# Attention with decay and a gated spatial block: weight conversion in larger blocks, later marks, two homes for operands, other sums

## Chip, cores and metric

The kernel runs on one NeuronCore of a Trainium2 chip. The metric is the device time of one execution in microseconds. Five engines work side by side, each through its own instructions in order: PE (matmul; its weight loads are listed as PEld), DVE (vector), ACT (scalar), POOL (GpSimd) and SP, which here only issues DMAs.

## The reference

Inputs are q, k, v of 8 batches x 8 heads x 576 positions x 64, a decay f, and the weights of a gated block. Cut to what is computed:

```python
scores = q @ k.T / 8 + (cum[:, None] - cum[None, :])     # cum = cumsum(log f), causal mask
attn = exp(scores - max); attn = attn / (sum(attn) + 1e-9)
x = (attn @ v), the 8 heads side by side                   # 576 x 512 per batch
h = relu(x @ w_in); u, v2 = h[:, :512], h[:, 512:]
v_n = (v2 - mean) / sqrt(var + 1e-6)
v_s = w_spatial @ v_n + b_spatial
out = (u * v_s) @ w_out                                    # 576 x 512 per batch
```

The weights `w_in` and `w_out` come as 64-bit floating point numbers.

## The kernel before

**Attention** goes by pairs of heads, 32 pairs P, four to a batch. For a pair and each of its two heads h, `scores(P, h)` multiplies four blocks of 128 queries by 128, 256, 384 and 512 keys into PSUM (tile `sc`); DVE scales, masks and takes the negated row maximum (L264, into `tt`, maximum `nm`), ACT takes the exponential with its row sum (L266, sum into `sm`), DVE adds 1e-9 to the sums and inverts them (L269, L270), and POOL multiplies `tt` by the inverse (L274). `scores_tail(P)` does the last 64 queries of both heads together in two halves of 288 keys (L285), whose maxima are joined by L289 before the exponential L290. `transposes` turns `tt` by PE (L320, tile `tp`), `evac` copies it to SBUF (L305 in float32, L309 and L310 in two parts), and `attend` multiplies by v (tile `x`) and writes the result as a high and a low part, `xh` and `xl` (L368, L369). In the program the scores of pair P+1 stand between the transposes of pair P, so the two interleave.

**Two kinds of operands.** Pairs 0 to 3 (`NQ`) use float32 score operands of 66 rows, tile `tf`: 64 rows of q and k and two decay rows from `r0`. Pairs from 4 on use two tiles `ta` and `tb` built by six DMAs per head from the parts `hi` and `lo` that `split` makes (L207, L210, L212), with decay rows from DRAM, written once by `split_rows` (L113). Pairs 0 to 4 (`NF`) have float32 attention weights `ef`, later ones `eh` and `el`.

**The gated block**, `moe(b)`, runs once per batch: five tiles through the second half of `w_in` (tiles `winh`, `winl`) with a normalisation each, then `u` through its first half, then the spatial product, then `w_out` (`woh`, `wol`). A loop hands out steps of attention and of `moe(b)` by estimated progress, with attention a quarter of a batch ahead.

**Weight conversion.** `load64` takes a block of 64-bit weights to two float32 parts: a DMA (L137), ACT for the absolute value (L141), five steps on DVE (L142, L144, L145, L147, L148), an addition on POOL (L149), ACT's copy to the high part (L150), POOL's subtraction for the low one (L151). `load_first` converts the second half of `w_in` in four blocks of 512 columns, and `w_spatial`, while pair 0 and 1 run. `load_rest` converts the first half of `w_in` in 8 blocks of 256 elements per partition before the first `moe`, and `w_out` in 8 such blocks inside `moe(0)`.

**What sets the order.** The program is written step by step, but a scheduler with its own estimates of duration places the instructions of every engine; `after(i, mark)` only keeps an instruction behind a marked earlier one. At the start PE runs 26 matmuls on a zero tile (`zm`).

Of the kernel before, what the change touches and what calls it, by code (L numbers as in the profile page):

```python
# [38 lines left out]
def attn_gmlp_kernel(ctx: ExitStack, tc: tile.TileContext, qk, v, f, w_in, w_sp, b_sp, w_out, out):  # L39
# [67 lines left out]
    def split_rows(ws, r0):  # L107
# [5 lines left out]
        SY.dma_start(out=rows_d[:], in_=f32(rt[:]))  # L113
# [21 lines left out]
    def load64(src, dh, dl, raw, w, a, mark=None):  # L135
# [5 lines left out]
        A.activation(af, hi.bitcast(F32), AF.Abs)  # L141
# [11 lines left out]
    def load_first(ws):  # L153

        for c in range(NJ):
# [25 lines left out]
    def load_rest(n, w_v, dh, dl, tag, bufs):  # L181

        raw = mo.tile([128, NJ, 64, 2], U32, name="w64", tag=("gt0", "gt1", "o")[n % 3], bufs=1)
        w = mo.tile([128, NJ, 64], U32, name="w32", tag=tag, bufs=bufs)
        t = mo.tile([128, NJ, 64], U32, name="wa", tag=tag, bufs=bufs)
        c = slice(64 * n, 64 * n + 64)
        load64(w_v[:, :, c, :], dh[:, :, c], dl[:, :, c], raw, w[:], t[:])
# [11 lines left out]

    vts, tab, parts, r0s = {}, {}, {}, []  # L200

    def split(P):
# [12 lines left out]
    def prep(P, h):  # L215

        p = slice(64 * h, 64 * h + 64)
        if P < NQ:
# [58 lines left out]
    def scores_tail(P):  # L277
        nm = wk.tile([128, 4], F32, name="nm", tag="nm", bufs=3)
        sm = wk.tile([128, 4], F32, name="sm", tag="sm", bufs=3)
        for j in range(2):  # L280
# [95 lines left out]
    def attention(b, ws=None):  # L376
        for P in range(b * PPB, (b + 1) * PPB):
            if P == 0:
# [235 lines left out]
```

## Time and profile before

| | |
|---|---|
| median of 3 runs | 815.25 us (813.65 to 815.45) |
| span of the profiled execution | 811.5 us |
| PE busy | 788.3 us (97%) |
| DVE, ACT, POOL busy | 567.1, 535.2, 478.1 us |

The profiled execution is known by its span from the first to the last instruction; the median of the timed runs lies 3.75 us above it. Busy PE time counts a matmul from its start to a modelled end, and ends overlap the next start, so a rate is read from the distance of starts.

### The profile page before, as it was taken

Reading aid. Unit: us, or ns where it says so; the run is one execution under the profiler, and the core shown is the slowest. Engines: PE = TensorE matmul, PEld = TensorE weight load, DVE = VectorE, ACT = ScalarE, POOL = GpSimd, SP = SyncE. Lnnn points to the kernel's source line nnn. Section 1 sums busy time; section 2 is a strip of 40 time slices with the busy share of each in tenths; the row PEclk is TensorE's granted clock in tenths of the full one; section 3 lists DMA queues with packets and bytes.
Section 4 is the critical chain, followed back from the end, with each engine's and each line's share of the span. In section 5 each row is a group of like instructions: output and inputs, shape, how many; then the busy total and the mean of one; then the engine's idle time right before and its main releaser. Section 6 shows DMA issues by size and latency. Waiting matters only on the chain.

```text
span 811.5 us, 15566 instructions
## 1 busy us (share of the span) xinstructions
PE 788.3 (97%) x4980; PEld 704.9 (87%) x4980; DVE 567.1 (70%) x1726; ACT 535.2 (66%) x1432; POOL 478.1 (59%) x677
## 2 busy tenths in 40 slices
PE   7999899999999999999999999999999999999997
PEld 3676678998899989998799989999899988999996
DVE  5879989676976668766776668776786658765321
ACT  5587668676776667666686667776687657764431
POOL 4767788655766647555775537566675547643151
PEclk8699999999999999999999999999999999999999
DMA  7547754456545554565554565556554664430001
GB/s 201 143 121 208 197 140 116 120 151 165 139 122 135 135 146 117 128 166 140 125 141 112 150 152 126 123 144 151 131 130 107 163 164 111 95 77 14 27 1 66
DMA packets 47476, 103.50 MB, mean 128 GB/s; under 512 B 6961, under 2 KB 15153, under 8 KB 47330
## 3 DMA queue, kind: packets, MB, share of 16 engines
q1 hardware_dynamic: 47074, 101.98, 49.8%
q8 instruction: 40, 0.66, 0.3%
q10 hardware_dynamic: 320, 0.52, 0.3%
q14 instruction: 42, 0.34, 0.1%
HBM read 39.41 MB, written 10.68 MB: 62 GB/s over the span
## 4 chain that ended last, share of the span: by engine, by line
PE 87%; DVE 5%; POOL 2%; ACT 2%; DMA 2%; issue 1%; SPq 0%; ACTq 0%; POOLq 0%; DVEq 0%
PE ps L198 47%; PE sc L198 16%; PE x L198 12%; PE tp L320 8%; PE tp L198 2%; PE tp L333 2%; DMA out_dram<-o 1%; POOL tt L274 1%; DVE w L145 1%; ACT tt L266 1%; DVE tt L264 1%; DVE eh L342 0%; DVE wa L142 0%; DVE ef L305 0%; DMA w<-in_dram 0%
## 5 line engine op out<-in xcount | busy, mean ns | idle before, releaser
L274 POOL TENSOR_SCALAR tt<-tt,sm 128x128 f32<-128x128 f32 (+3 forms) x256 | 138.3, 558 | 94.7 <-DVE sm L270 86.4
L264 DVE CUSTOM_DVE_ANT_0 tt<-sc,zm 128x128 f32<-128x128 f32 (+3 forms) x256 | 122.4, 485 | 82.4 <-PE tp L320 63.0
L309 ACT CAST eh<-tp 128x512 fp32r<-128x512 f32 (+1 forms) x270 | 111.5, 425 | 87.2 <-PE tp L320 52.5
L266 ACT ACTIVATE tt<-tt,nm 128x128 f32<-128x128 f32 (+3 forms) x256 | 144.4, 565 | 26.5 <-DVE nm L264 21.5
L310 DVE TENSOR_TENSOR el<-tp,eh 128x512 fp32r<-128x512 f32 (+1 forms) x270 | 127.9, 485 | 25.0 <-ACT eh L309 22.8
L320 PE MATMUL tp<-ident,tt 128*128 128x128 f32 x640 | 113.7, 280 | 1.3 <-DVE ef L305 0.6
L198 PE MATMUL sc<-ta 128*128 128x128 f32 (+1 forms) x336 | 107.8, 327 | 3.9 <-DVE nm L264 3.8
L198 PE MATMUL x<-eh,vt 128*128 128x320 f32 (+4 forms) x378 | 104.5, 287 | 2.7 <-POOL vt L243 1.8
L198 PE MATMUL sc<-tb 68*128 68x128 f32 (+1 forms) x336 | 104.6, 316 | 0.0
L212 POOL TENSOR_TENSOR lo<-raw,hi 128x640 fp32r<-128x640 f32 (+1 forms) x56 | 83.2, 1506 | 18.5 <-ACT hi L210 18.4
L505 POOL TENSOR_TENSOR gl<-u,gh 128x256 fp32r<-128x256 f32 x64 | 47.2, 738 | 79.3 <-ACT gh L504 76.1
L198 PE MATMUL x<-el,vt 128*128 128x256 f32 x324 | 93.4, 306 | 0.0
L320 PEld LDWEIGHTS tp<-ident,tt 128*128 128x128 f32 x640 | 76.8, 142 | 10.9 <-ACT ef L305 1.2
L198 PEld LDWEIGHTS x<-eh,vt 128*128 128x128 f32 x378 | 71.2, 189 | 5.8 <-POOL vt L243 2.7
L198 PE MATMUL ps<-sph,vnh 128*128 128x256 f32 (+1 forms) x240 | 73.3, 306 | 0.2 <-ACT o L530 0.2
L198 PE MATMUL ps<-sph,vnl 128*128 128x256 f32 (+1 forms) x240 | 71.4, 298 | 0.0
L198 PEld LDWEIGHTS sc<-ta 128*128 128x128 f32 x336 | 63.5, 189 | 9.1 <-DVE nm L264 4.9
L198 PE MATMUL ps<-spl,vnh 128*128 128x256 f32 (+1 forms) x240 | 71.2, 296 | 0.0
L198 PE MATMUL ps<-xh,winh 128*128 128x256 f32 (+1 forms) x232 | 70.1, 302 | 0.1
L198 PE MATMUL ps<-xl,winh 128*128 128x256 f32 (+1 forms) x232 | 68.9, 297 | 0.0
L368 ACT CAST xh<-x 64x256 fp32r<-64x256 f32 (+1 forms) x128 | 49.8, 392 | 28.4 <-PE x L198 26.9
L198 PE MATMUL ps<-xh,winl 128*128 128x256 f32 (+1 forms) x232 | 68.4, 295 | 0.0
(190 smaller groups left out, 2127.8 us busy)
## 6 DMA issues: line engine op xcount, KB each, us to landing
raw<-in_dram SPq DMA_DIRECT2D x28, 608.0 KB
ta<-hi SPq DMA_DIRECT2D x56, 304.0 KB
vraw<-in_dram SPq DMA_DIRECT2D x32, 320.0 KB
tb<-hi SPq DMA_DIRECT2D x56, 160.0 KB
ta<-lo SPq DMA_DIRECT2D x56, 160.0 KB
out_dram<-o SPq DMA_DIRECT2D x32, 256.0 KB
ta<-hi SPq DMA_DIRECT2D x56, 144.0 KB
tb<-lo SPq DMA_DIRECT2D x56, 144.0 KB
```

The costliest lines, as they stand in the source:

```text
L145: V.scalar_tensor_tensor(out=w, in0=hi, scalar=0xC0000000, in1=a, op0=ALU.bitwise_and, op1=ALU.bitwise_or)
L198: T.matmul(o, l, r, start=st, stop=sp)
L212: G.tensor_tensor(out=lo[:, c], in0=raw[:, c], in1=f32(hi[:, c]), op=ALU.subtract)
L264: V.tensor_tensor_reduce(out=t, in0=sc[:, 0:n], in1=zm[:, 640 - n:640], scale=-0.125, scalar=3.0e38, op0=ALU.add, op1=ALU.min, accum_out=n ...
L266: last["exp", P, h, i] = A.activation(t, t, AF.Exp, bias=nm[:, i:i + 1], scale=-1.0, accum_out=sm[:, i:i + 1])
L274: G.tensor_scalar(out=t, in0=t, scalar1=sm[:, i:i + 1], scalar2=1.0, op0=ALU.mult, op1=ALU.mult)
L309: A.copy(h_ap, ps)
L310: V.tensor_tensor(out=l_ap, in0=ps, in1=f32(h_ap), op=ALU.subtract)
L320: T.transpose(out=tp[:, (i - c) * 128:(i - c + 1) * 128], in_=tt[h][:, TOFF[i] + 128 * c:TOFF[i] + 128 * c + 128], identity=ident)
L333: T.transpose(out=tp[:, j * 128:(j + 1) * 128], in_=tl[:, c * 128:(c + 1) * 128], identity=ident)
L368: last[P, h] = A.copy(hi, ps[m0:m0 + 64, 0:n])
L505: G.tensor_tensor(out=gl[j][:, 0:256], in0=g[:, 0:256], in1=f32(gh[j][:, 0:256]), op=ALU.subtract)
```

## The change

- `load_rest` converts the first half of `w_in` in 2 blocks of 1024 elements per partition (a pool `wu` of its own, ahead of the pool `mo`), and `w_out` in 4 blocks of 512, whose raw tile shares the tile `gt` and whose work tiles share the two `vx` buffers. The two `gt` tiles become one.
- In `load_first`, ACT's first step of block 0 stands behind the last exponential of the first head (`("exp", 0, 0, 3)`), that of the other blocks behind the second exponential of the second head; the first step of this generator is held back by 0.033.
- `split_rows` stands behind the loads of pair 1, and its DMA behind `("exp", 0, 1, 0)`. The unused call `split(1)` goes. The DMA of `raw` gets the mark `("exp", P - 2, 0, 3)`, that of the decay rows of `tb` the mark `("exp", P - 1, 0, 0)`.
- The float32 operands `tf` of even pairs live in the buffers of `ta`, those of odd pairs in those of `tb`, so that pair 1 can load while pair 0 is in use.
- The row sums go to three constant tiles `se` of 4 x 2 whose second column holds 1e-9 from the start; one TENSOR_REDUCE adds the two columns in place of L269. The second half of the tail takes the first half's maximum as its starting value, and L289 goes.

The core of the diff:

```diff
-        SY.dma_start(out=rows_d[:], in_=f32(rt[:]))
+        after(SY.dma_start(out=rows_d[:], in_=f32(rt[:])), ("exp", 0, 1, 0))
...
-        A.activation(af, hi.bitcast(F32), AF.Abs)
+        after(A.activation(af, hi.bitcast(F32), AF.Abs), behind)
...
+                   ("exp", 0, 0, 3) if c == 0 else ("exp", 0, 1, 1))
...
+    sums = [cst.tile([128, NB, 2], F32, name=f"se{n}") for n in range(3)]
+    for t in sums:
+        G.memset(t, 1.0e-9)
...
-        SY.dma_start(out=raw, in_=qk[P])
+        after(SY.dma_start(out=raw, in_=qk[P]), ("exp", P - 2, 0, 3))
...
-            ta = wk.tile([66, QK], F32, name="tf", tag="ta", bufs=2)
+            ta = wk.tile([66, QK], F32, name="tf", tag="ta" if P % 2 == 0 else "tb", bufs=2)
...
-        SY.dma_start(out=f32(tb[64:68, :]), in_=rows_v[:, P, h, :])
+        after(SY.dma_start(out=f32(tb[64:68, :]), in_=rows_v[:, P, h, :]), ("exp", P - 1, 0, 0))
...
-                                                accum_out=sm[:, i:i + 1])
+                                                accum_out=se[:, i, 0:1])
...
-        V.tensor_scalar(out=sm, in0=sm, scalar1=1.0e-9, scalar2=None, op0=ALU.add)
+        V.tensor_reduce(out=sm, in_=se, op=ALU.add, axis=AX.X)
...
-                                   in1=zm[:, 0:288] if j == 0 else zm[:, 640:928], scale=-0.125, scalar=3.0e38,
+                                   in1=zm[:, 0:288] if j == 0 else zm[:, 640:928], scale=-0.125,
+                                   scalar=nm[:, 0:1] if j else 3.0e38,
...
-        V.tensor_tensor(out=nm[:, 2:3], in0=nm[:, 0:1], in1=nm[:, 1:2], op=ALU.min)
...
-                split_rows(ws, r0s[0])
-                split(1)
...
+            if P == 0:
+                split_rows(ws, r0s[0])
...
-            for n in range(8):
-                load_rest(n, wo_v, woh, wol, 'GH', 3)
+            for n in range(4):
+                raw = mo.tile([128, NJ, 128, 2], U32, name="w64", tag="gt")
+                w, a = (mo.tile([128, NJ, 128], U32, name=k, tag="vx", bufs=2) for k in ("w32", "wa"))
+                load_rest(wo_v, woh, wol, slice(128 * n, 128 * n + 128), raw, w, a)
...
-        da, dw = 0.0, 0.0
+        da, dw = 0.0, 0.033
...
+    with tc.tile_pool(name="wu", bufs=2, reuse_waits="tile") as wu:
+        for n in range(2):
+            raw = wu.tile([128, NJ, 256, 2], U32, name="w64")
+            w, a = (wu.tile([128, NJ, 256], U32, name=k) for k in ("w32", "wa"))
+            load_rest(win_v, winh, winl, slice(256 * n, 256 * n + 256), raw, w, a)
```

Since the scheduler places everything anew, the order changes in many places. Three of them:

DVE at the start, before: from the memsets of `rt` (decay rows) to the fourth score block of pair 0, head 0 (`tt_94`); `wa` and `w_...` belong to the weight conversion.

```order
L85 MEMSET rt 32x4x64 x2
L142 TENSOR_SCALAR wa<-wa 128x512
L144 TENSOR_SCALAR wa<-wa 128x512
L264 ISA tt_94,nm<-sc,zm 128x128
L264 ISA nm 128x1
L145 SCALAR_TENSOR_TENSOR w_177<-w_176,wa 128x512
L142 TENSOR_SCALAR wa<-wa 128x512
L264 ISA tt_94,nm<-sc,zm 128x256
L264 ISA nm 128x1
L147 TENSOR_SCALAR wa<-w_177 128x512
L264 ISA tt_94,nm<-sc,zm 128x384
```

The same place after (L268 is the old L264, L289 the old L285, L273 the new sum):

```order
L85 MEMSET rt 32x4x64 x2
L268 ISA tt_94,nm<-sc,zm 128x128
L268 ISA nm 128x1
L268 ISA tt_94,nm<-sc,zm 128x256
L268 ISA nm 128x1
L268 ISA tt_94,nm<-sc,zm 128x384
L268 ISA nm 128x1
L268 ISA tt_94,nm<-sc,zm 128x512
L268 ISA nm 128x1
L289 ISA tl,nm<-sc,zm 128x288
L289 ISA nm 128x1
L273 TENSOR_REDUCE sm<-se_101 128x4
```

The conversion steps that stood ahead of the first score block, and between the blocks, now stand behind all four and the first half of the tail.

PE before, from the last score block of pair 0 to the first product with v (`x_335`); the blocks 128 and 256 behind the 512 belong to pair 1:

```order
L198 MATMUL sc<-tf 128x512
L198 MATMUL sc<-tf 128x128
L198 MATMUL sc<-tf 128x256
L320 MATMUL tp<-ident,tt_94 128x128 x3
L198 MATMUL sc<-tf 128x384
L320 MATMUL tp<-ident,tt_94 128x128 x6
L198 MATMUL sc<-tf 128x512
L198 MATMUL sc<-tf 128x288 x4
L320 MATMUL tp<-ident,tt_94 128x128
L198 MATMUL x_335<-ef,vraw 128x256
```

The same place after, from the second score block of pair 0, head 1:

```order
L195 MATMUL sc<-tf 128x256
L324 MATMUL tp<-ident,tt_94 128x128
L195 MATMUL sc<-tf 128x384
L324 MATMUL tp<-ident,tt_94 128x128 x2
L195 MATMUL sc<-tf 128x512
L195 MATMUL sc<-tf 128x128
L324 MATMUL tp<-ident,tt_94 128x128 x6
L195 MATMUL sc<-tf 128x256
L195 MATMUL sc<-tf 128x384
L195 MATMUL sc<-tf 128x512
L324 MATMUL tp<-ident,tt_94 128x128
L195 MATMUL x_339<-ef,vraw 128x256
```

The first transposes stand among the scores of pair 0 itself, and the first product with v stands ahead of the tail of pair 1 (the four 288s) where it stood behind it.

SP before, the loads of the first half of `w_in` (`w_945` and on, 256 KB each) and the first operands of pair 4:

```order
L137 DMA w_945<-in_dram 128x4x128
L137 DMA w_958<-in_dram 128x4x128
L137 DMA w_971<-in_dram 128x4x128
L220 DMA tf<-in_dram 64x1216
L221 DMA tf<-r_114 2x1x1216
L137 DMA w_984<-in_dram 128x4x128
L237 DMA vraw<-in_dram 128x640
L137 DMA w_997<-in_dram 128x4x128
L230 DMA tb<-hi 64x640 x2
L227 DMA ta<-hi 64x1216
```

The same place after, from `raw` of pair 4:

```order
L209 DMA raw<-in_dram 128x1216
L178 DMA sptb<-bs_820 1x16x36
L179 DMA sptb<-bs_821 1x16x36
L137 DMA w_937<-in_dram 128x4x512
L137 DMA w_950<-in_dram 128x4x512
L239 DMA vraw<-in_dram 128x640
L229 DMA ta<-hi 64x1216
L231 DMA ta<-hi 64x576
L229 DMA ta<-hi 64x1216
L230 DMA ta<-lo 64x640
```

Two loads of 1 MB each now stand in one piece ahead of `vraw` of pair 2 and the operands of pair 4.

## Rows read from the trace of the kernel before

**Rows 1.** The page's first lines: the span, and PE's busy time, share and instructions.

```profile
span 811.5 us, 15566 instructions
PE 788.3 (97%) x4980; PEld 704.9 (87%) x4980; DVE 567.1 (70%) x1726; ACT 535.2 (66%) x1432; POOL 478.1 (59%) x677
```

**Rows 2.** Busy time of each engine by stretch: stretch and its length, then busy us and instructions of PE, PEld, DVE, ACT, POOL, then the granted TensorE clock as a share of 2.4 GHz, the DMA share and GB/s. The stretches end where the warm-up ends, where the clock falls, where it rises, at 70 us, at the first matmul of `moe(0)`, when `w_out` is converted and in use, and before the end.

```profile
0.00:9.60 9.60, 7.64 (x26) 2.92 (x27) 4.03 (x8) 4.90 (x8) 8.03 (x19) 1.00 0.67 185
9.60:12.40 2.80, 1.54 (x6) 0.88 (x6) 0.00 (x0) 1.65 (x4) 0.00 (x0) 1.00 0.99 338
12.40:36.30 23.90, 22.56 (x53) 14.71 (x53) 19.34 (x54) 11.76 (x33) 14.15 (x15) 0.50 0.57 145
36.30:70.00 33.70, 33.08 (x164) 24.13 (x164) 28.34 (x94) 26.60 (x74) 23.59 (x29) 1.00 0.50 143
70.00:97.30 27.30, 22.61 (x111) 15.50 (x109) 25.45 (x87) 18.75 (x55) 21.77 (x29) 1.00 0.81 211
97.30:165.00 67.70, 64.63 (x412) 57.86 (x412) 56.85 (x157) 45.10 (x120) 51.52 (x69) 1.00 0.52 129
165.00:725.00 560.00, 555.14 (x3711) 514.95 (x3710) 401.42 (x1251) 393.29 (x1059) 332.39 (x476) 1.00 0.55 135
```

**Rows 3.** The timeline of all engines in the first 45 us: start, duration, engine, line, operation, tiles, form, count, and in brackets the idle time before it with its releaser.

```profile
9.61 1.54 PE L198 MATMUL sc<-tf 66*128 66x128 f32 x6 [0.18 <-DMA tf<-r]
...
11.90 0.66 ACT L141 ACTIVATE wa<-w 128x512 f32<-128x512 f32 x1 [1.14 <-DMA w<-in_dram]
12.59 0.43 DVE L142 TENSOR_SCALAR wa<-wa 128x512 f32<-128x512 f32 x1 [5.01 <-ACT wa L141]
...
13.39 0.28 DVE L264 CUSTOM_DVE_ANT_0 tt<-sc,zm 128x128 f32<-128x128 f32 x1
...
13.74 11.46 PE L198 MATMUL sc<-tf 66*128 66x512 f32 x22 [2.59 <-DVE nm L264]
...
19.77 1.26 POOL L151 TENSOR_TENSOR winl<-w,winh 128x512 fp32r<-128x512 f32 x1 [0.73 <-ACT winh L150]
...
20.39 0.67 DVE L269 TENSOR_SCALAR sm<-sm 128x4 f32<-128x4 f32 x1
...
24.99 0.84 PE L320 MATMUL tp<-ident,tt 128*128 128x128 f32 x3
...
33.95 1.06 PE L198 MATMUL x<-ef,vraw 128*128 128x256 f32 x2
```

**Rows 4.** The timeline of PE around 60 us, at full clock. A float32 matmul is recorded as two.

```profile
58.23 1.02 PE L198 MATMUL sc<-tf 66*128 66x512 f32 x2
59.09 0.39 PE L198 MATMUL x<-ef,vraw 128*128 128x128 f32 x2
59.31 0.93 PE L320 MATMUL tp<-ident,tt 128*128 128x128 f32 x7
60.08 1.78 PE L198 MATMUL x<-ef,vraw 128*128 128x320 f32 x6
```

**Rows 5.** Groups of instructions, shapes kept apart: the conversion steps of the 16 blocks of 256. Busy us and mean ns of one behind the first bar, idle before it behind the second.

```profile
L149 POOL TENSOR_TENSOR w<-w,wa 128x256 f32<-128x256 f32 x16 | 12.7, 792 | 13.3 <-DVE sm L269 6.7 <-DVE wa L148 5.0 <-DVE sm L270 1.6
L142 DVE TENSOR_SCALAR wa<-wa 128x256 f32<-128x256 f32 x16 | 9.6, 603 | 2.9 <-ACT wa L141 2.9
L145 DVE SCALAR_TENSOR_TENSOR w<-w,wa 128x256 uint32<-128x256 uint32 x16 | 9.5, 591 | 0.3
L144 DVE TENSOR_SCALAR wa<-wa 128x256 uint32<-128x256 uint32 x16 | 8.8, 548 | 0.1
L148 DVE SCALAR_TENSOR_TENSOR wa<-w,wa 128x256 f32<-128x256 uint32 x16 | 8.6, 536 | 0.1
L147 DVE TENSOR_SCALAR wa<-w 128x256 uint32<-128x256 uint32 x16 | 6.8, 425 | 0.1
```

**Rows 6.** Single conversion steps in the timelines of DVE and POOL: short ones of 256 and of 512, and one that ran beside a POOL instruction.

```profile
27.29 0.69 DVE L145 SCALAR_TENSOR_TENSOR w<-w,wa 128x512 uint32<-128x512 uint32 x1
30.10 0.42 DVE L142 TENSOR_SCALAR wa<-wa 128x512 f32<-128x512 f32 x1
68.04 3.13 POOL L212 TENSOR_TENSOR lo<-raw,hi 128x640 fp32r<-128x640 f32 x2
68.76 1.15 DVE L148 SCALAR_TENSOR_TENSOR wa<-w,wa 128x256 f32<-128x256 uint32 x1
73.04 0.41 DVE L145 SCALAR_TENSOR_TENSOR w<-w,wa 128x256 uint32<-128x256 uint32 x1
73.72 0.28 DVE L142 TENSOR_SCALAR wa<-wa 128x256 f32<-128x256 f32 x1
```

**Rows 7.** Groups of instructions: the two small DVE steps that go.

```profile
L269 DVE TENSOR_SCALAR sm<-sm 128x4 f32<-128x4 f32 x64 | 16.8, 262 | 9.6 <-ACT tt L266 9.0
L289 DVE TENSOR_TENSOR nm<-nm 128x1 f32<-128x1 f32 x32 | 8.9, 277 | 0.0
```

**Rows 8.** The timeline of PE at 270 us: four transposes, and the matmuls behind them.

```profile
269.82 0.60 PE L320 MATMUL tp<-ident,tt 128*128 128x128 f32 x4
270.18 0.39 PE L198 MATMUL ps<-sph,vnl 128*128 128x320 f32 x1
270.41 0.31 PE L198 MATMUL ps<-sph,vnh 128*128 128x320 f32 x1
270.56 0.31 PE L198 MATMUL ps<-spl,vnh 128*128 128x320 f32 x1
```

More of the change, by code (lines that the diff above doesn't have):

```diff
@@ L133, in after, with load64 @@
                 mybir.DependencyClass.NoSync, mybir.DependencyReason.DATA), reason="order")
-    def load64(src, dh, dl, raw, w, a, mark=None):
+    def load64(src, dh, dl, raw, w, a, mark=None, behind=None):
         after(SY.dma_start(out=raw, in_=src), mark)
@@ L158, in load_first @@
             t = ws.tile([128, DM], U32, name="wa")
-            load64(win_v[:, c, DM:2 * DM, :], winh[:, c, DM:2 * DM], winl[:, c, DM:2 * DM], raw, w[:], t[:], ("dma", 0, 1))
+            load64(win_v[:, c, DM:2 * DM, :], winh[:, c, DM:2 * DM], winl[:, c, DM:2 * DM], raw, w[:], t[:], ("dma", 0, 1),
+                   ("exp", 0, 0, 3) if c == 0 else ("exp", 0, 1, 1))
             yield 500
@@ L179, in load_first, with load_rest @@
         yield 500
[L181 to L187, printed above, removed]
+    def load_rest(w_v, dh, dl, c, raw, w, a):
+        load64(w_v[:, :, c, :], dh[:, :, c], dl[:, :, c], raw, w[:], a[:])
     tt = [cst.tile([128, 1280], F32, name=f"tt{h}") for h in range(2)]
@@ L198, in mm @@
         T.matmul(o, l, r, start=st, stop=sp)
+    sums = [cst.tile([128, NB, 2], F32, name=f"se{n}") for n in range(3)]
+    for t in sums:
+        G.memset(t, 1.0e-9)
+    nsum = [0]
     vts, tab, parts, r0s = {}, {}, {}, []
@@ L256, in scores @@
         nm = wk.tile([128, 4], F32, name="nm", tag="nm", bufs=3)
+        se = sums[nsum[0] % 3]
+        nsum[0] += 1
         sm = wk.tile([128, 4], F32, name="sm", tag="sm", bufs=3)
@@ L480, in moe @@
         if b == 0:
-            for n in range(8):
-                load_rest(n, wo_v, woh, wol, 'GH', 3)
+            for n in range(4):
+                raw = mo.tile([128, NJ, 128, 2], U32, name="w64", tag="gt")
+                w, a = (mo.tile([128, NJ, 128], U32, name=k, tag="vx", bufs=2) for k in ("w32", "wa"))
+                load_rest(wo_v, woh, wol, slice(128 * n, 128 * n + 128), raw, w, a)
         if b % 2 == 0:
-            gt[0] = [mo.tile([128, NJ, 128], F32R, name=f"gt{r}", tag=f"gt{r}") for r in range(2)]
+            gt[0] = mo.tile([128, 2, NJ, 128], F32R, name="gt", tag="gt")
         r0 = 64 * (b % 2)
@@ L506, in moe @@
                 if t0:
-                    th, tlo = (gt[0][r][:, j, r0:r0 + 64] for r in range(2))
+                    th, tlo = (gt[0][:, r, j, r0:r0 + 64] for r in range(2))
                     A.copy(th, g[:, 256:320])
@@ L513, in moe @@
         if b % 2 == 1:
-            yield from w_out_tile(b, *[[g[:, j, :] for j in range(NJ)] for g in gt[0]],
+            yield from w_out_tile(b, *[[gt[0][:, r, j, :] for j in range(NJ)] for r in range(2)],
                                   [(b - 1, TL, 0, 64), (b, TL, 64, 64)])
@@ L559, in attn_gmlp_kernel @@
     ps_m = ctx.enter_context(tc.tile_pool(name="ps_m", bufs=2, space=PSUM, reuse_waits="tile"))
-    for n in range(8):
-        load_rest(n, win_v, winh, winl, 'U', 9)
     for b in range(B):
```

2 lines of the change are left out of this document (1 added, 1 removed).

## Prediction

> **What bounds the kernel now.** I read the page's first lines, then busy time by stretch, then timelines of the stretches where PE falls behind. PE is busy for 97% of the span [rows 1]; from 165 to 725 us for 555.1 of 560.0 us at full clock [rows 2]. There only fewer or cheaper PE instructions help, and the change leaves PE's work as it is. So I look for what PE loses ahead of 165 us.
>
> PE's work there is priced from distances of starts at full clock [rows 4]: a float32 matmul of 512 columns takes 59.09 - 58.23 = 0.86 us (1.68 ns a column), a transpose (60.08 - 59.31) / 7 = 0.11 us. A pair has 2 x 1280 + 1152 = 3712 score columns, 3200 columns in its product with v, and 25 transposes. Four pairs cost 4 x 3712 x 1.68 ns = 24.9, 4 x 3200 x 1.68 ns = 21.5 and 100 x 0.11 = 11.0 us; with some 3.4 us for pair 4's cheaper scores, 61 us stand ahead of the first matmul of `moe(0)`. Scores begin at 9.6 us and `moe(0)` at 97.3 [rows 2, 3]: 87.7 us, so 27 us are lost. They fall into two parts.
>
> First, 9.6 to 36.3 us. PE stops for 2.59 us until 13.74, since DVE has not drained the first score block; DVE sits idle for 5.01 us behind the ACT step of a weight block whose DMA came late, and the conversion stands ahead of the block in DVE's order [rows 3]. The clock falls to 0.50 (1.2 GHz) at 12.4 and stays there until 36.3 [rows 2]. In these 26.7 us PE does 12.6 us worth of work (the matmuls of 9.61 to 11.15, 1.3 us worth, and half of 22.6 busy us): 14 us are lost.
>
> Second, 36.3 to 97.3 us: 61 us for 48.3 us of work, 12.7 lost, some 9 of them behind 70 us. There DVE is busy for 25.45 of 27.3 us while PE has 22.61, and the DMA share is 0.81 [rows 2]. A conversion block of 256 costs DVE 603 + 591 + 548 + 536 + 425 = 2703 ns [rows 5], where short ones are 3 x 0.28 + 2 x 0.41 = 1.66 us; the difference, 1.04 us a block, is waiting: L148 took 1.15 us beside two long POOL subtractions, against 0.41 for a step of its size [rows 6].
>
> **The change part by part.**
>
> *Start.* DVE now drains the first score blocks as they come, and the stop of 2.59 us goes. PE then has 2.8 us of work done at 12.4 where it had 1.3. What follows depends on the clock. Before, it fell at 12.4, 1.3 us into the stop, and rose at 36.3, 2.35 us after the first product with v (33.95) [rows 3]. Score matmuls alone had not raised it: PE worked without a stop from 13.74 to about 25.2, all of it at 0.50 [rows 2, 3]. Behind the warm-up the new order holds 4.7 us of scores ahead of its first transpose, and the first product with v stands at 9.4 us of work instead of 11.4. I take it that the clock falls again. Half speed then reaches that product at 12.4 + 2 x (9.4 - 2.8) = 25.6 us. If the clock rises 2.35 us later, PE has 10.6 us done at 28 and passes 12.6 at 30, 6.3 us sooner than before; if only at 36.3, it has 2.8 + 23.9 / 2 = 14.8 us done there, 2.2 ahead. I take 4, bounds 2 to 6.3.
>
> The loads of pair 1, 2 x 304 KB, stand where the load of `raw`, 608 KB, stood, and the DMA share is 0.67 up to 9.6 us [rows 2]: between 0 and 1 us of delay for the first score, taken as 0. POOL is busy for 8.03 of those 9.6 us [rows 2], which leaves room for the three small memsets of `se`. `split_rows` keeps its place on ACT, and its DMA of 1.2 MB leaves the stretch of 9.6 to 12.4 us, where the DMA share is 0.99 [rows 2].
>
> *First half of `w_in`.* A step of 512 takes 0.42 or 0.69 us, so 256 elements add 0.14 and 0.28 [rows 6]. A step of 1024 costs 0.70 or 1.25 us, a block 3 x 0.70 + 2 x 1.25 = 4.6, two blocks 9.2 against 8 x 1.66 = 13.3 us. Waits were 0.21 us a step; 10 steps instead of 40 save 6.3 us if they stay so, but POOL's pieces grow. Two subtractions of 640 and 576 take 3.13 us [rows 6], so one of 1024 some 2.5 us against 0.79 for 256 [rows 5], and a step behind it can lose as much. At 0.6 a step the waits are 6 us against 8.3. DVE saves some 6 us. But the blocks are dense: by the order their ten steps fall into about 15 us of PE work, with a pair's own 10 us of DVE, and the second half of the second half of `w_in` moves into this stretch too (2 x 2.7 us). Of 12.7 us lost I give back 2, bounds -3 to +6.
>
> The Trainium skill, SBUF — State Buffer, section Who interferes with whom, has DVE and GpSimd take one port pair as an exclusive lock, for DVE instructions with two SBUF inputs or a two-port mode, so that whoever comes second waits for the whole of the other. The 1.15 us above agree. By that rule longer POOL pieces speak against this change: each of the ten steps could lose up to 2.5 us, 25 us in all, and the term would be -3 at the least instead of +2.
>
> *`w_out`.* Four blocks at 3 x 0.42 + 2 x 0.69 = 2.64 us of short steps, 10.6 against 13.3, and 20 waits instead of 40; DVE saves 2.7 + 2 to 4 us, and the two last blocks of `w_in` that ran behind 97.3 are gone. DVE is busy for 56.9 of 67.7 us there and PE loses about 5 [rows 2]. Against it, each block holds both `vx` buffers and the one raw buffer, so the blocks come one by one, and the first `w_out` matmul, which needs all four, stands 7.7 us of work later on PE. I take +2, bounds -4 to +4.
>
> *Sums and maxima.* L269 is 16.8 and L289 8.9 us of DVE [rows 7]; a TENSOR_REDUCE of 4 x 2 is not in the trace, its price lies between the shortest small step and L269's mean, 0.15 to 0.26 us, so between 0 and 7 us of DVE go with L269 and 8.9 with L289. From 165 us on DVE is busy for 401 of 560 us [rows 2], so it costs or brings nothing there; before that it is in the terms above.
>
> *Steady order.* The matmul behind a run of transposes starts 0.23 us ahead of its successor where the next has 0.15 [rows 8]: some 0.08 us a switch. The order holds 314 runs of transposes before and 289 now: 25 x 0.08 = 2.0 us. The marks on `raw` and on the decay rows leave a pair's time ahead of use, some 23 us (560 us for six batches of four pairs [rows 2]). I take +2, bounds -2 to +4.
>
> **Sum.** 4 + 2 + 2 + 2 = 10 us: the span goes from 811.5 to 801.5. The median lies 3.75 us above the span, so I forecast 805.25, say 805.
>
> **The rivals.**
>
> *The clock stays up.* With no stop behind the warm-up, PE may hold 2.4 GHz. Then 12.6 us of work end at 9.6 + 12.6 + 1 = 23.2 instead of 36.3, 13 us sooner; but ACT, POOL and DVE don't get faster, and `load_first` now falls into less time, so I count 12, and 1 instead of 2 in the second part: 12 + 1 + 2 + 2 = 17, 798. For it: from 36.3 to 70 us, with 0.6 us of stops in all, the clock stayed at 1.00 [rows 2]. Against it: those 11.5 us at 0.50 without a stop. The Trainium skill, TensorE: Matmul & The Clock Gate, Part 1, says that sustained matmul activity lifts the halved clock and idleness brings it back; by that the unbroken start would stay up, and this rival would be the forecast. The row of 13.74 speaks against the plain form of the rule.
>
> *DVE sets the time to `moe(0)` anyway.* DVE is busy for 77 of the first 97.3 us [rows 2]; what PE gains at the start it then waits for in the dense blocks: 4 - 3 + 0 + 2 = 3, 812.
>
> *Slower: pair 4 comes late.* SP has two 1 MB loads in one piece ahead of `vraw` of pair 2 and the operands of pair 4, which came in 256 KB pieces. At 211 GB/s [rows 2] 2 MB take 10 us. The order leaves about 12 us of PE work between them and `vraw`'s use; if SP comes to them some 8 us late, PE stops for 8 us, the clock falls as it did in a stop of 2.59 us, and as long at half speed as before costs 12 more: 8 + 12 - 10 = 10 us slower, 825. It turns slower once a stop passes about 3 us and takes the clock with it.
>
> **How the numbers follow.** Forecast 0.47, clock up 0.27, DVE-bound 0.16, slower 0.10. 0.2% of the median is 1.6 us, about what a measurement can tell from no change. The forecast and the clock rival are faster; of the DVE case 0.10 is faster and 0.06 the same. So faster 0.84, same 0.06, slower 0.10. The forecast's own terms reach from 805 - 5 to 805 + 6; for 8 in 10 the range takes in most of the clock rival and of the DVE case: 794 to 813.
>
> **What would show it.** Right: no stop at 11 us, the first score block drained before 10.5; a clock that falls near 12.4 and rises between 28 and 36; `moe(0)` at some 90 to 92 us; conversion steps of 1024 at 0.7 to 1.3 us and their waits; runs from 165 on of the same length but for 2 us. Wrong: no fall of the clock (798); `moe(0)` at 95 or later with DVE full (812); PE waiting for DMAs of `vraw`, `ta` or `tb` ahead of 90 us (slower).

## The result and the profile after

The changed kernel takes 820.1 us (median of 15 runs, 813.5 to 820.8) where the kernel before takes 813.96 (15 runs beside them, 813.0 to 815.5): a ratio of 1.0053, 95% interval 1.0036 to 1.0070. It is slower by half a per cent. The forecast was faster, and the time lies above the range. Executions of one kernel lie several us apart with what the clock does in them (the changed kernel's go from 813.5 us at a mean granted clock of 0.988 to 820.8 at 0.976), so a difference of some 3 us between two medians is weak.

The page's first lines after, to be held against [rows 1]:

```profile
span 819.0 us, 15454 instructions
PE 794.7 (97%) x4980; PEld 711.0 (87%) x4980; DVE 548.6 (67%) x1644; ACT 536.7 (66%) x1412; POOL 478.8 (58%) x660
```

VectorE has 18.5 us less to do, as the change meant, and the span is 7.5 us longer. Two parts of a span can be read off: the stops of PE (span less PE's busy time) and the time lost to the halved clock (span times one less the mean granted clock, which the view of the cores gives as 0.985 before and 0.976 after).

| | span | stops | lost to the clock | rest |
|---|---|---|---|---|
| before | 811.5 | 23.2 | 12.2 | 776.1 |
| after | 819.0 | 24.3 | 19.7 | 775.0 |

So in the sum the difference is clock: 19.7 - 12.2 = 7.5 us. (Some 0.9 us of it cost nothing: the clock is at 0.82 from 814 us to the end, where PE has no more work.) Where, busy time by stretch shows (columns as in [rows 2], the same stretches without the first):

```profile
9.60:12.40 2.80, 1.39 (x5) 1.09 (x6) 0.61 (x3) 1.35 (x5) 0.00 (x0) 0.86 0.82 252
12.40:36.30 23.90, 23.90 (x67) 15.90 (x65) 15.07 (x52) 12.27 (x35) 6.87 (x10) 0.59 0.50 131
36.30:70.00 33.70, 30.99 (x136) 21.71 (x136) 25.91 (x74) 23.84 (x64) 28.98 (x32) 0.90 0.49 163
70.00:97.30 27.30, 24.96 (x133) 19.09 (x133) 25.02 (x72) 20.82 (x52) 22.04 (x19) 1.00 0.81 198
97.30:165.00 67.70, 63.65 (x409) 57.05 (x408) 50.46 (x143) 45.47 (x114) 51.08 (x63) 0.97 0.56 142
165.00:725.00 560.00, 553.42 (x3667) 512.41 (x3666) 390.52 (x1205) 389.25 (x1043) 330.68 (x469) 0.99 0.53 133
```

Before, the clock was at 0.50 once and at 1.00 from 36.3 us on [rows 2]. Now the first low stretch is 11.6 to 32.1 us, 1.7 us cheaper than 12.4 to 36.3, and there are three new ones: 52.6 to 59.4, 131.1 to 134.5 and 168.6 to 175.5 us. Half of 6.8 + 3.4 + 6.9 us is 8.6 us lost. These are the places in PE's timeline after:

```profile
11.01 4.51 PE L195 MATMUL sc<-tf 66*128 66x128 f32 x9 [1.97 <-DMA tf<-r]
...
29.34 1.06 PE L195 MATMUL x<-ef,vraw 128*128 128x256 f32 x2
...
52.57 0.79 PE L195 MATMUL sc<-tf 66*128 66x128 f32 x2 [1.69 <-DVE nm L268]
...
130.69 0.40 PE L195 MATMUL sc<-ta 128*128 128x288 f32 x1 [1.57 <-DVE nm L268]
...
161.94 0.33 PE L195 MATMUL sc<-ta 128*128 128x128 f32 x1 [0.77 <-DVE nm L289]
...
166.36 0.44 PE L195 MATMUL sc<-ta 128*128 128x384 f32 x1 [0.90 <-DVE nm L268]
...
168.34 0.41 PE L324 MATMUL tp<-ident,tt 128*128 128x128 f32 x2 [0.56 <-DVE el L314]
...
170.78 1.18 PE L195 MATMUL ps<-woh,gh 128*128 128x512 f32 x2
```

The stop of 2.59 us [rows 3] is gone, but one of 1.97 us stands ahead of the first score, and the clock falls behind that. The first product with v comes 4.6 us earlier than in [rows 3]; a stop at 51 us takes the clock again, and `moe(0)` begins at 96.24 us, 1.1 us earlier. That stop stands behind a conversion step on VectorE, which took 1.78 us beside two subtractions on GpSimd; the same step took 0.69 us at 166.90 us. The score block that PE waits for comes behind it in VectorE's order.

```profile
49.17 1.78 DVE L148 SCALAR_TENSOR_TENSOR wa<-w,wa 128x512 f32<-128x512 uint32 x1
```

```profile
46.99 3.42 POOL L166 TENSOR_TENSOR spl<-wraw,sph 128x576 fp32r<-128x576 f32 x2
```

From 156 to 170 us PE has attention alone, since no `w_out` tile can begin before all four blocks are converted, and it stops again and again for VectorE. The first `w_out` matmul, 157.35 us before, comes at 170.78. Its cause in GpSimd's timeline after, the last step of each of the four blocks:

```profile
138.17 1.29 POOL L151 TENSOR_TENSOR wol<-w,woh 128x512 fp32r<-128x512 f32 x1
...
146.34 1.29 POOL L151 TENSOR_TENSOR wol<-w,woh 128x512 fp32r<-128x512 f32 x1 [0.73 <-ACT woh L150]
...
162.06 1.27 POOL L151 TENSOR_TENSOR wol<-w,woh 128x512 fp32r<-128x512 f32 x1
...
170.75 1.28 POOL L151 TENSOR_TENSOR wol<-w,woh 128x512 fp32r<-128x512 f32 x1 [1.39 <-ACT woh L150]
```

and the same step of the eighth block in the kernel before, 26 us earlier:

```profile
145.07 0.74 POOL L151 TENSOR_TENSOR wol<-w,woh 128x256 fp32r<-128x256 f32 x1
```

How far PE has come shows what each part cost. This is an estimate from the two traces: every matmul counts for its median distance to the next at full clock, 752 us in all behind the zeros.

| PE's work done, us | reached before, us | reached after, us | after is |
|---|---|---|---|
| 22 | 47.5 | 44.7 | 2.8 ahead |
| 32 | 57.7 | 60.3 | 2.6 behind |
| 62 (just ahead of `moe(0)`) | 95.7 | 94.7 | 1.0 ahead |
| 102 | 140.1 | 138.6 | 1.5 ahead |
| 132 | 170.7 | 178.8 | 8.1 behind |
| 752 | 805.5 | 813.5 | 8.0 behind |

The start does bring something, the stop at 51 us takes it back, and the whole loss that remains stands where `w_out` is converted.

### The profile page after: what moved, and what is told of

Same layout as the page of the kernel before. It is cut to its first block, busy times and chain, and to the rows that moved or that the text cites. A ratio compares the mean times of both kernels' runs of the same rounds, so it can differ in the third digit from the quotient of the medians.

```text
span 819.0 us, 15454 instructions
## 1 busy us (share of the span) xinstructions
PE 794.7 (97%) x4980; PEld 711.0 (87%) x4980; DVE 548.6 (67%) x1644; ACT 536.7 (66%) x1412; POOL 478.8 (58%) x660
## 4 chain that ended last, share of the span: by engine, by line
PE 85%; DVE 6%; DMA 3%; POOL 2%; ACT 2%; issue 1%; POOLq 0%; DVEq 0%; ACTq 0%; SPq 0%
PE ps L195 45%; PE sc L195 17%; PE x L195 12%; PE tp L324 8%; PE tp L195 2%; PE tp L337 2%; DVE tt L268 1%; DMA w<-in_dram 1%; DMA tb<-hi 1%; DVE vx L460 1%; DVE el L314 1%; DVE w L145 1%; POOL tt L278 0%; DMA out_dram<-o 0%; DVE xl L373 0%
## 5 line engine op out<-in xcount | busy, mean ns | idle before, releaser
L268 DVE CUSTOM_DVE_ANT_0 tt<-sc,zm 128x128 f32<-128x128 f32 (+3 forms) x256 | 122.7, 487 | 114.3 <-PE tp L324 73.9
L195 PE MATMUL x<-el,vt 128*128 128x256 f32 x324 | 91.6, 307 | 0.4 <-DVE el L314 0.4
L373 DVE TENSOR_TENSOR xl<-x,xh 64x256 fp32r<-64x256 f32 (+1 forms) x128 | 57.4, 451 | 19.0 <-ACT xh L372 16.8
```

Source lines behind the costliest of these rows:

```text
L195: T.matmul(o, l, r, start=st, stop=sp)
L268: V.tensor_tensor_reduce(out=t, in0=sc[:, 0:n], in1=zm[:, 640 - n:640], scale=-0.125, scalar=3.0e38, op0=ALU.add, op1=ALU.min, accum_out=n ...
L373: V.tensor_tensor(out=lo, in0=ps[m0:m0 + 64, 0:n], in1=f32(hi), op=ALU.subtract)
```

## The experiments

A *home* is a buffer, or a set of them, that a tile is placed in; a *stop* is time in which PE has nothing to run. Theory A: four `w_out` blocks one by one through `vx` and one raw buffer end late, `moe(0)` has no matmuls left to give PE, and the clock falls. Theory B: the loss is in the first 70 us. Each run is timed against the kernel before on its chip (814.2 to 814.8 us); ratios are with 95% intervals.

**1. `w_out` as before, in the changed kernel** (the two `gt` tiles with it).

```diff
-            for n in range(4):
-                raw = mo.tile([128, NJ, 128, 2], U32, name="w64", tag="gt")
-                w, a = (mo.tile([128, NJ, 128], U32, name=k, tag="vx", bufs=2) for k in ("w32", "wa"))
+            for n in range(8):
+                raw = mo.tile([128, NJ, 64, 2], U32, name="w64", tag=("gt0", "gt1", "o")[n % 3], bufs=1)
+                w, a = (mo.tile([128, NJ, 64], U32, name=k, tag="GH", bufs=3) for k in ("w32", "wa"))
```

> The changed kernel with one part undone: w_out is converted in eight blocks of 64 columns as before (raw in three homes, work tiles in 'GH'). Theory A (four w_out blocks, each holding both 'vx' buffers and the one raw buffer, end some 26 us of the span later; moe(0) then has no w_out tile to give, TensorE is left with attention alone, waits for VectorE and the clock falls at 131 and 169 us): the fall at 168.6 us is gone, the first w_out matmul comes at about 155 us and the time is 810 to 814 us, 6 to 10 us below the changed kernel. Theory B (the loss stands in the first 70 us, the stop at 52.6 us and the second clock fall): 818 to 821 us, no change against the changed kernel.

814.37 us (807.8 to 816.2), ratio 0.9981 (0.9957 to 1.0006): 5.7 us below the changed kernel, level with the kernel before. In its trace the first `w_out` matmul comes at 161.24 us, later than A said but 9.5 us sooner than in the changed kernel, and the clock stays at 1.00 behind 100 us.

```profile
161.24 0.64 PE L195 MATMUL ps<-woh,gh 128*128 128x512 f32 x2
```

So A holds for nearly all that is lost against the kernel before, though the time is 0.4 us above its range. But all the rest of the change, put at 8 us, is worth 1.5 by the ratio, and that is not clear of nothing.

**2 and 3. The kernel before with two `w_in` blocks, and with four `w_out` blocks too.**

```diff
+    with tc.tile_pool(name="wu", bufs=2, reuse_waits="tile") as wu:
+        for n in range(2):
+            raw = wu.tile([128, NJ, 256, 2], U32, name="w64")
+            w, a = (wu.tile([128, NJ, 256], U32, name=k) for k in ("w32", "wa"))
+            load_rest(win_v, winh, winl, slice(256 * n, 256 * n + 256), raw, w, a)
...
-    for n in range(8):
-        load_rest(n, win_v, winh, winl, 'U', 9)
```

> The kernel before with one part of the change alone: the first half of w_in converted in two blocks of 256 columns of each of the four chunks, ahead of the pool mo. Theory A: 812 to 814 us, since the start stays and w_out too; moe(0) starts about a microsecond earlier at most. Theory B: 814 to 817 us, because larger steps on VectorE and GpSimd hold attention up at 70 to 97 us.

> The run above (two w_in blocks) and w_out in four blocks through 'vx' with them; the start as in the kernel before. Theory A: 818 to 822 us, 5 to 9 us above the run with the two w_in blocks alone, with a clock fall between 130 and 180 us. Theory B: within 2 us of the run with the two w_in blocks alone.

821.62 us, ratio 1.0095 (1.0078 to 1.0112), and 834.13, ratio 1.0239 (1.0221 to 1.0257). Both lie above every range. `w_out` costs 12.5 us here, twice as much as in run 1; the first `w_out` matmul comes at 171.1 us in run 2 and at 191.3 in run 3. `w_in` alone costs 7.4, which neither theory said. VectorE and GpSimd of the run with `w_in` alone, at 72 us:

```profile
72.79 2.88 DVE L145 SCALAR_TENSOR_TENSOR w<-w,wa 128x1024 uint32<-128x1024 uint32 x1
```

```profile
72.24 2.35 POOL L149 TENSOR_TENSOR w<-w,wa 128x1024 f32<-128x1024 f32 x1 [1.16 <-DVE wa L148]
75.74 2.35 POOL L151 TENSOR_TENSOR winl<-w,winh 128x1024 fp32r<-128x1024 f32 x1 [1.16 <-ACT winh L150]
```

The step on VectorE begins 0.55 us into GpSimd's and ends 1.1 us behind it, which is about the 1.25 us that the prediction gave it without a wait. A copy of transposes stands behind it, PE stops for 2.35 us, and the clock falls there and again at 121 us, behind a stop of 1.27 us; the two falls cost 6.8 us. Whether the second comes from these blocks is not shown. The Trainium skill, SBUF — State Buffer, section Who interferes with whom, makes the port pair an exclusive lock held for a whole instruction; 2.88 us beside a piece of 2.35 agrees.

**4. The changed kernel without the marks on the first conversions**, and without the hold-back of 0.033 on them.

```diff
-            load64(win_v[:, c, DM:2 * DM, :], winh[:, c, DM:2 * DM], winl[:, c, DM:2 * DM], raw, w[:], t[:], ("dma", 0, 1),
-                   ("exp", 0, 0, 3) if c == 0 else ("exp", 0, 1, 1))
+            load64(win_v[:, c, DM:2 * DM, :], winh[:, c, DM:2 * DM], winl[:, c, DM:2 * DM], raw, w[:], t[:], ("dma", 0, 1))
...
-    da, dw = 0.0, 0.033
+    da, dw = 0.0, 0.0
```

> The changed kernel without the marks that hold the first four conversions of w_in behind an exponential of pair 0, and with dw starting at 0 as before (the decay rows and the later marks stay as changed). Theory A: still 817 to 821 us, since the w_out part is untouched. Theory B (pushing the first conversions back fills GpSimd at 40 to 60 us, TensorE stops at 52.6 us and the clock falls for 7 us): the clock stays up at 52 to 60 us and the time is 813 to 817 us.

823.44 us, ratio 1.0109 (1.0091 to 1.0127). The clock does stay up at 52 to 60 us, as theory B has it, but the time is 3 us longer and not 3 to 7 shorter: the stop behind the first scores is back (2.02 us ahead of 14.15 us), and low stretches come at 40, 80 and 162 us instead. So undoing the marks is no remedy; what the stop at 51 us costs by itself, this run does not tell.

**5. Small blocks in the changed kernel's homes.**

```diff
-            for n in range(4):
-                raw = mo.tile([128, NJ, 128, 2], U32, name="w64", tag="gt")
-                w, a = (mo.tile([128, NJ, 128], U32, name=k, tag="vx", bufs=2) for k in ("w32", "wa"))
+            for n in range(8):
+                raw = mo.tile([128, NJ, 64, 2], U32, name="w64", tag="gt")
+                w, a = (mo.tile([128, NJ, 64], U32, name=k, tag="vx", bufs=2) for k in ("w32", "wa"))
```

> The changed kernel with w_out in eight blocks of 64 columns, as small as before, but still through the homes of the changed kernel: the raw block in 'gt' (one buffer), the work tiles in 'vx' (two buffers). Theory A1 (the loss of w_out is the one-by-one order: each block holds all homes until GpSimd's last subtraction of it): as slow as the changed kernel or slower, 819 to 826 us, since eight blocks one by one take longer than four. Theory A2 (the loss is the length of the single steps on VectorE and GpSimd, 1.2 to 2.4 us with 512 numbers a row, in front of which scores wait): 813 to 816 us, like the run with the old conversion of w_out.

843.96 us, ratio 1.0335 (1.0301 to 1.0370): 30 us above run 1, which has the same eight blocks in more homes. So what makes `w_out` late is the homes, not the length of a step, as A1 says, though its range ended at 826. Eight blocks one by one are worse than four, and their last one ends at 221 us:

```profile
220.47 0.74 POOL L151 TENSOR_TENSOR wol<-w,woh 128x256 fp32r<-128x256 f32 x1
```

**6. Both conversions as before, in the changed kernel** (the edit of run 1, and that of run 2 turned round).

> The changed kernel with both block conversions (w_in's first half and w_out) as before; what is left of the change is the order at the start, the two homes of the float32 operands and the sums and maxima. Larger steps cost (w_in's two blocks alone cost 7 us on the kernel before): 805 to 809 us, below both kernels. Rival (in the changed start the first conversions are out of the way, so w_in's blocks fall into a slacker place and cost nothing there): 812 to 815 us, as with w_out alone undone.

817.66 us, ratio 1.0024 (1.0003 to 1.0044): neither forecast. The two `w_in` blocks, which cost 7.4 us on the kernel before, save 3.3 us here (817.66 - 814.37), though the intervals of runs 1 and 6 just touch. The price of an edit hangs on the rest. What is left of the change without the two conversions (start, marks, homes, sums) is 2 us slower than the kernel before, where the prediction's terms for it are 4 + 2 us faster.

**7. The kernel before with the joined sums and maxima alone.**

```diff
-            last["exp", P, h, i] = A.activation(t, t, AF.Exp, bias=nm[:, i:i + 1], scale=-1.0,
-                                                accum_out=sm[:, i:i + 1])
+            last["exp", P, h, i] = A.activation(t, t, AF.Exp, bias=nm[:, i:i + 1], scale=-1.0,
+                                                accum_out=se[:, i, 0:1])
-        V.tensor_scalar(out=sm, in0=sm, scalar1=1.0e-9, scalar2=None, op0=ALU.add)
+        V.tensor_reduce(out=sm, in_=se, op=ALU.add, axis=AX.X)
...
-        V.tensor_tensor(out=nm[:, 2:3], in0=nm[:, 0:1], in1=nm[:, 1:2], op=ALU.min)
```

> The kernel before with the joined sums and tail maxima alone (the 1e-9 comes in through a second column of the sum, the second tail minimum starts from the first). Two VectorE steps of some 0.1 us per pair fewer or shorter and a chain per tail that is one step shorter, in a stretch where TensorE is busy for 99%: 813 to 815 us, no change. Rival: the shorter chain spares TensorE stops in the pairs of the second half, 809 to 812 us.

821.35 us, ratio 1.0079 (1.0066 to 1.0091): outside both ranges; an edit that does little but take work from VectorE costs 7 us. The timeline of ScalarE, and PE's behind it:

```profile
95.24 0.41 ACT L150 CAST winh<-w 128x256 fp32r<-128x256 f32 x1 [0.29 <-POOL w L149]
103.03 0.43 ACT L141 ACTIVATE wa<-w 128x256 f32<-128x256 f32 x1 [7.38 <-DMA w<-in_dram]
103.49 0.59 ACT L312 COPY ef<-tp 128x512 f32<-128x512 f32 x1
```

```profile
104.13 0.44 PE L327 MATMUL tp<-ident,tt 128*128 128x128 f32 x2 [2.37 <-ACT ef L312]
```

ScalarE stands for 7.38 us in front of a weight block that is still on the way. A copy that PE waits for stands behind it in the same queue; PE stops for 2.37 and then 1.20 us and the clock is at 0.50 from 104.6 to 111.5 us. It also falls at 84.2 us for 3.4 us, behind a stop of 1.08 us for a load of `ta`. The scheduler's new order has it so.

**8. One home for the float32 operands, in the changed kernel.**

```diff
-            ta = wk.tile([66, QK], F32, name="tf", tag="ta" if P % 2 == 0 else "tb", bufs=2)
+            ta = wk.tile([66, QK], F32, name="tf", tag="ta", bufs=2)
```

> The changed kernel with the float32 operands of pairs 0 and 1 in one home of two buffers, as before, so that the loads of pair 1 wait until the scores of pair 0 are done. Theory A (the two homes put pair 1's loads into the queue with pair 0's and make the first score 1.4 us later, but take out the stop of 2.6 us at 11 us): first score back at 9.6 us, a stop of 2 to 3 us in front of pair 1's scores, 819 to 823 us. Rival (the homes only shift the start): 817 to 819 us.

821.82 us, ratio 1.0094 (1.0081 to 1.0107): inside A's range, for another reason. The first score comes at 10.25 us without a stop, pair 1's with stops of 0.6 and 0.9 us, and **the clock does not fall** until 28 us; `moe(0)` begins at 87.2 us, 9 us earlier. It is all lost again at the four `w_out` blocks. VectorE, GpSimd and PE of this run:

```profile
148.31 4.84 DVE L142 TENSOR_SCALAR wa<-wa 128x512 f32<-128x512 f32 x1
153.08 0.41 DVE L314 TENSOR_TENSOR el<-tp,eh 128x256 fp32r<-128x256 f32 x1
```

```profile
146.53 1.57 POOL L245 TENSOR_TENSOR vt<-vraw,vt 128x640 fp32r<-128x640 f32 x1
148.04 2.93 POOL L214 TENSOR_TENSOR lo<-raw,hi 128x640 fp32r<-128x640 f32 x2
150.92 1.27 POOL L151 TENSOR_TENSOR wol<-w,woh 128x512 fp32r<-128x512 f32 x1
152.14 0.73 POOL L511 TENSOR_TENSOR gl<-u,gh 128x256 fp32r<-128x256 f32 x1
```

```profile
153.64 0.66 PE L337 MATMUL tp<-ident,tl 128*128 128x128 f32 x2 [4.24 <-DVE el L314]
```

A step of 0.42 us [rows 6] takes 4.84 and ends as GpSimd's unbroken run ends; PE stops for 4.24 us behind it. The same step of `w_out` took 4.32 us in run 3 and 4.89 in run 5, each beside such a run, with stops of 4.23 and 5.58 us behind it.

**9 and 10. The stop ahead of the first score filled**, in the changed kernel and in that of run 1. The nine more matmuls of zeros do nothing else.

```diff
-                for _ in range(26):
+                for _ in range(35):
```

> The changed kernel with 35 instead of 26 warming matmuls of zeros ahead of the first score, which fill the 2 us in which TensorE waits there for the loads and do nothing else (if they outlast the loads, the first score is at most 0.7 us later). Theory C (a stop of some 2 us is what takes the clock away, and each fall costs about half its length): the fall at 11.6 to 32 us is gone, mean granted clock 0.985 to 0.99, 809 to 813 us, 8 to 11 us below the changed kernel. Rival (the clock falls at about 11 us whatever TensorE did just before): clock and time as in the changed kernel, 819 to 821 us.

> The changed kernel with w_out's conversion as before and 35 warming matmuls. If both prices add up (6 us for w_out, 8 to 10 us for the fall at the start): 803 to 807 us, below the kernel before by 1% or more. Rival (an earlier start only moves the later stops, at which the clock then falls): 810 to 814 us.

813.76 us, ratio 0.9992 (0.9980 to 1.0003), and 809.7, ratio 0.9936 (0.9924 to 0.9948). Busy time of run 9 in two stretches, which the low one of 12.4 to 36.3 us fell into before:

```profile
9.60:30.00 20.40, 19.76 (x92) 13.20 (x90) 13.47 (x52) 13.11 (x38) 7.99 (x11) 1.00 0.77 203
30.00:40.00 10.00, 6.53 (x17) 4.49 (x18) 6.63 (x20) 6.93 (x19) 8.84 (x9) 0.66 0.49 146
```

Work that is worth nothing brings 6.3 us in run 9 and 4.7 in run 10 (against run 1), since the clock stays up to 30 us: theory C holds on the clock, but its 809 to 813 us are missed. But a stop of 4.07 us (4.46 in run 10) at 30 us then takes the clock for 7 us, and the full 8 to 10 us do not come: run 10 lies between its two ranges, and the later stop is what its rival named. The Trainium skill, TensorE: Matmul & The Clock Gate, Part 1, has idleness bring the halved clock and sustained matmuls lift it; both runs agree with the first half.

```profile
33.47 2.50 PE L195 MATMUL sc<-tf 66*128 66x512 f32 x4 [4.07 <-DVE nm L268]
```

In run 9 the clock falls twice more, at 149 and 162 us, while `w_out` is converted; in run 10, with `w_out` as before, it does not, and that is worth 4.1 us. Run 10 is the fastest kernel of this study, 4.6 us below the one before.

**11. `w_out` as before and one home** (the edits of runs 1 and 8).

> The changed kernel with w_out's conversion as before and one home for the float32 operands. In the run with one home alone the first score came at 10.25 us without a stop and the clock stayed up until 28 us, but TensorE stopped for 4.2 and 3.6 us between 149 and 170 us. Theory A (those two stops are w_out's one-by-one blocks): they go with the old conversion and 806 to 811 us remain. Rival (the stops come from the moved order of attention, not from w_out): 817 to 822 us.

811.84 us (808.7 to 816.2), ratio 0.9967 (0.9952 to 0.9982), 10 us below run 8: the two stops behind 149 us are gone, as A says, with a time just above its range. One of 3.17 us at 125.6 us is left and takes the clock with it. No conversion step made it: VectorE's step of the normalisation (L460) took 5.33 us beside another unbroken run of GpSimd, and the score block stands behind it. VectorE, GpSimd and PE:

```profile
122.95 5.33 DVE L460 TENSOR_SCALAR vx<-vx,mv 64x512 f32<-64x512 f32 x1 [0.93 <-POOL mv L459]
```

```profile
122.89 2.93 POOL L214 TENSOR_TENSOR lo<-raw,hi 128x640 fp32r<-128x640 f32 x2
125.79 1.52 POOL L245 TENSOR_TENSOR vt<-vraw,vt 128x640 fp32r<-128x640 f32 x1
127.28 0.72 POOL L151 TENSOR_TENSOR wol<-w,woh 128x256 fp32r<-128x256 f32 x1
```

```profile
128.80 0.61 PE L195 MATMUL sc<-ta 128*128 128x288 f32 x1 [3.17 <-DVE nm L268]
```

**12. `w_out`, sums and maxima as before** (the edits of run 1, and of run 7 turned round).

> The changed kernel with w_out's conversion and the sums and maxima as before; the order at the start, the two homes and w_in's two blocks stay. On the kernel before the joined sums alone cost 7 us, because ScalarE stood for 7.4 us in front of a w block's load with a transposes' copy behind it and the clock fell twice. Theory D (that price hangs on where the planner then puts the conversion steps, not on the sums): no fixed gain, 811 to 817 us. Rival (the joined sums cost by themselves): 805 to 809 us.

817.33 us, ratio 1.0043 (1.0023 to 1.0062), just above theory D's range: the joined sums that cost 7 us on the kernel before save 3 here (817.33 - 814.37).

**13. The third conversion behind the scores**, on top of run 10. There ScalarE waited 4.75 us for the third block's load, from 25.1 us on, VectorE waited for ScalarE, and PE for VectorE:

```profile
29.87 0.66 ACT L141 ACTIVATE wa<-w 128x512 f32<-128x512 f32 x1 [4.75 <-DMA w<-in_dram]
```

```profile
30.63 0.43 DVE L142 TENSOR_SCALAR wa<-wa 128x512 f32<-128x512 f32 x1 [4.10 <-ACT wa L141]
```

```profile
34.05 1.22 PE L195 MATMUL sc<-tf 66*128 66x512 f32 x1 [4.46 <-DVE nm L268]
```

```diff
-                   ("exp", 0, 0, 3) if c == 0 else ("exp", 0, 1, 1))
-            yield 500
+                   (("exp", 0, 0, 3), ("exp", 0, 1, 1), ("exp", 1, 1, 1), ("exp", 1, 1, 3))[c])
+            yield 500 if c != 1 else 1000
```

> The changed kernel with w_out's conversion as before, 35 warming matmuls, and the third and fourth conversion of w_in's second half moved behind the second and the last exponential of pair 1's second half, so that they stand behind the scores instead of before them. In the run without this move ScalarE stood 4.75 us in front of the third block's load, VectorE behind ScalarE and TensorE behind VectorE for 4.5 us, and the clock fell for 7 us. Theory F (a conversion step that stands ahead of scores in an in-order queue, while its block is still on the way, is what makes the stop): the stop of 4.5 us and the fall at 33 us are gone, 801 to 806 us. Rival (the vector work itself is too much there, wherever it stands): a stop of 2 us or more within the next 20 us and 808 to 812 us.

812.54 us (810.6 to 815.4), ratio 0.9974 (0.9961 to 0.9987): slower than run 10. F is right on the place: the stop of 4.46 us and the fall behind it are gone. The time is near the rival's, but its stop of 2 us within 20 us does not come: a stop of 1.4 us at 40 us takes the clock, and between 66 and 135 us six stops of 1.3 to 2.1 us follow, for ScalarE's copies and VectorE's minima. Lost to the clock in the profiled executions: 3.3 us as in run 10 (0.996 in both); stops: 813.5 - 783.8 = 29.7 against 807.5 - 783.0 = 24.5 us. (The profiled execution of run 13 took 815.29 us.)

## Why the prediction was wrong

- **The step that failed is the `w_out` term, +2 with -4 as its lower end.** It named the mechanism, "the blocks come one by one", had the first `w_out` matmul 7.7 us of work later, and then priced only VectorE's savings against it. Measured: that matmul comes 13.4 us later, the changed kernel falls 9.6 us back between 102 and 132 us of work, and the blocks lose 5.7 us in it (run 1), 12.5 on the kernel before with two `w_in` blocks (runs 2 and 3), 10.0 with one home (runs 8 and 11) and 4.1 with more zeros (runs 9 and 10). Run 5 shows that the shared homes are it. Left out was what PE does meanwhile: with no `w_out` tile to run, it has attention alone, at VectorE's pace, and loses the clock.
- **Start, +4: the gain came and went.** This is the other part of the miss: 6 us were to be gained by `moe(0)`, and 1.1 came. The stop of 2.59 us went, the first product with v came 4.6 us earlier, the clock rose at 32 us, and at 22 us of work the changed kernel is 2.8 us ahead, within the bounds. Then the stop at 51 us, with the fall behind it, takes 5.4 us. The prediction has no such term: the conversion steps that now stand behind the first scores still stand ahead of later ones, and one waited there beside GpSimd.
- **The loads of pair 1, taken as 0 and bounded by 1 us.** SP issues `tf<-r` no later than before (6.92 us against 7.05), but it now stands behind those loads, the DMA share is 0.98 from 4 to 11 us, and the first score comes 1.4 us later (9.61 us in [rows 3], 11.01 now). In run 11, which has those loads later, the share is 0.54 from 4 to 9.3 us and the first score comes at 9.33; in run 8, at 10.25, as the zeros end. Filling this stop brought 6.3 and 4.7 us (runs 9 and 10).
- **"The clock falls again"** was right for the wrong reason: a stop took it, not the scores that follow. Without a stop of 1 us or more it stayed up to 28 us and more (runs 8 to 11), the sign by which the prediction would have known its clock rival.
- **First half of `w_in`, +2 with -3 to +6.** Without `w_out` in blocks, +3.3 in the changed kernel (run 6) and -7.4 alone on the kernel before: the range held the first only. The rule on the lock, weighed as -3 or worse, fits the second: its first stop stands behind a step that waited so.
- **VectorE sets the time to `moe(0)`.** This rival's sign came: `moe(0)` at 96.24, later than 95. Its cause did not: in runs 8 to 11 and 13 VectorE has the same two `w_in` blocks ahead of `moe(0)`, which yet begins at 87.2 to 91.1 us. What held it was the lost clock and single stops, not the amount of VectorE's work.
- **Steady order, +2.** From 132 us of work to the end the changed kernel goes from 8.1 to 8.0 us behind. Term: 0.
- **Sums and maxima, 0.** Wrong on the kernel before: -7, of which 4.7 us stand in the first 170 us by the same estimate. In the changed kernel +3 (runs 7 and 12). Which it is goes with the order that the scheduler makes of it.
- **The slower rival** had the right ending, a stop that takes the clock, in the wrong place: the loads of pair 4 stop PE for 0.45 and `vraw` for 0.67 us. By its own sum, 12 us for the fall against 10 gained, any stop that takes the clock turns the kernel slower, not only one of 3 us.
- **From span to median, 3.75 us.** In the single executions of the changed kernel the time lies 1.8 us above the span; the rest of the 3.75 was a profiled execution quicker than the median beside it. A span of 801.5 meant some 803 us.

What is not settled: which stop takes the clock. One of 1.35 us in the kernel before (PE's timeline, ahead of 94.86 us) did not, one of 1.57 ahead of 130.69 us after did; in run 13 one of 2.10 did not; in run 8 the fall at 28.1 us has only stops of 0.63 and 0.92 us ahead of it. Why the same edit costs on one kernel and saves in another is argued from the order, not shown. And that the place of the weight step in run 7 made its loss was read off its order and not tried.

## What to carry to other kernels

- Count the homes, not only the steps: a block that holds every buffer of its kind until its last instruction makes the next one's load wait, and the consumer that needs all blocks comes late by the sum. Ask what the busiest engine has to do until then.
- In-order engines: look for each step that waits for a load and ask what stands behind it. A weight step in front of its load held a copy, the copy held PE, and PE lost its clock; that is worth more than the step.
- Near the limit of two engines at once, parts of a change do not add up: each of two edits gave -7 us on one kernel and +3 on another. Price them in the kernel in which they will stand, and try filling a short stop with work before moving everything else.

## What the runs showed of the hardware

- A VectorE step of 512 elements with one SBUF input, 0.42 us alone, took 4.84 us (run 8). It began in the second of five GpSimd subtractions that follow each other without a gap, the longest of them 1.57 us, and ended 0.3 us behind the last. So its wait spans several instructions, not one; steps in runs 3, 5 and 11 took 4.32, 4.89 and 5.33 us in the same way. The Trainium skill, SBUF — State Buffer, section Who interferes with whom, has the loser wait for the other's whole instruction; here it waits for more than that.
- Nine matmuls of zeros, 2.2 us of TensorE, brought 6.3 us in run 9 and 4.7 in run 10: the clock, which had fallen at 11.6 us, stayed at 1.00 until 32 us.
